# LayerNorm 2 writes its features in an order of five blocks of 2x64, and the gate and up weights are loaded in the same row order

## The chip, the cores and the metric

One core of a Trainium2 chip. The metric is the device time of one execution in microseconds (us), the median of several runs. Engines in the profile: PE is TensorE, PEld its weight loads, DVE is VectorE, ACT is ScalarE, POOL is GpSimd, and SP is the engine that issues nearly all DMA transfers, SPq its queue. In the names, `ps` is a bank in which PE leaves its results, `pa` and `pd` hold the softmax exponents made by ACT and by DVE (with GpSimd's adds), and a product `ps<-qT,kT` makes scores.

## The reference

A transformer block with one key and value head, and a gated feed-forward part, in bf16:

```python
x  : [1, 2048, 640]          # 32 query heads of 20, one K and one V head
h  = x + attention(layernorm(x)) @ wo          # softmax(q k^T / sqrt(20)) v
h2 = h + (gelu(LN(h) @ w_gate) * (LN(h) @ w_up)) @ w_down      # 640 -> 1536 -> 640
# all weights ~ N(0,1) * 0.05; w_gate, w_up, w_down also * (rows ** -0.5)
```

Both LayerNorms are without scale and shift. The product `LN(h) @ w_gate` sums over the 640 features, so the features may stand in any order as long as the rows of the weights stand in the same one.

## The kernel before

The kernel is built by a greedy planner. It keeps a modelled clock for each engine, takes the next task that its model says can start, and so fixes the order of every engine's instructions when the program is built. On the chip each engine works through its own list and waits on semaphores (DVE's stop of 6.53 us below shows what that can cost). A modelled duration that is wrong makes no wrong result. It only makes an order that doesn't suit the chip, and any changed figure can change the order of everything after it.

The normalise step of both LayerNorms (`ln` is 0 or 1, `t` the tile of 128 rows; 16 tiles each):

```python
tk = _Task(("dve",), None, 420, L_DVE, keys + [("lr", kk)], [], prio, then, gate)   # 420 ns in the plan
def bind():
    s = start()
    tk.fn = lambda e: e.tensor_scalar(xn_tmp[:, s, :].rearrange("p (a b) -> p a b", a=5),
                xh[:, t, :], mv[:, ln, t, 0:1], ln_r[:, ln, t:t + 1], ALU.subtract, ALU.mult)
    tk.writes = [("xt", s)]
...
# then a DMA transposition [128 rows, 640] -> [128, 5, 128 rows], issued by SP
sp_tasks.append(_Task(("sp",), lambda e: e.dma_start_transpose(o, xn_tmp[:, s, :]), ...))
```

A task with `lock` set is planned as one that needs GpSimd idle: it starts after the GpSimd instruction in flight, and GpSimd's next starts after it. No wait is emitted for it.

```python
def commit(self, eng, fn, cost, lat, reads=(), writes=(), at=0.0, dma=False, lock=False):
    ...
    t0 = max([self.free[eng], at] + [o.vis for o in deps])
    if lock:
        for o in self.ops["pool"][-2:]:
            if o.t0 <= t0 < o.end:
                t0 = o.end
        self.port = t0 + cost
    elif eng == "pool":
        t0 = max(t0, self.port)
    ...
```

The weights of the output and feed-forward products come in pieces, one after the other: each piece is planned, and waits on the chip, until the piece before it has landed. All are issued by SP:

```python
w_pieces = []
for nm, o, v, n in (("wo", wo_sb, A_wo, 2), ("wg", wg_sb, B_w_gate, 4), ("wu", wu_sb, B_w_up, 4), ("wd", wd_sb, B_w_down, 4)):
    rows = o.shape[1]                       # wg_sb, wu_sb: [128 partitions, 5, 1536]
    cut = [rows * i // n for i in range(n + 1)]
    w_pieces += [(nm, i, o[:, x:y, :], cview(v)[:, x:y, :]) for i, (x, y) in enumerate(zip(cut, cut[1:]))]
for k, (nm, i, o, v) in enumerate(w_pieces):
    sp_tasks.append(_Task(("sp",), (lambda o, v: lambda e: e.dma_start(o, v))(o, v), 560, W_LAT,   # W_LAT = 3000 ns
        [w_pieces[k - 1][:2]] if k else [], [(nm, i)], ...))     # reads the key of the piece before
```

The softmax here doesn't subtract the row's maximum and nothing guards it: scores larger than these inputs give would overflow.

## Time and profile before

| | before |
|---|---|
| median, six runs | 775.96 us (774.23 to 776.50) |
| profiled run | 775.0 us |
| first exponent on ACT starts, last one ends | 13.86 us, 745.78 us |
| ACT busy between these, idle between these | 711.28 us, 20.65 us |
| after ACT's last exponent | 29.25 us |

ACT computes most of the softmax exponents, DVE with GpSimd the others. The four parts (until the first exponent, busy, idle, after the last exponent) add up to the span. They are summed over all records of ACT in the trace. The busy shares, the time lines of one LayerNorm pair and the durations of the line that changes are shown in the prediction.

### The profile page before, as it was taken

To read this page: it belongs to the slowest core of one execution; us is meant where nothing else is said; L and a number is where in the kernel's file an instruction comes from. 1 tells how busy PE (TensorE), PEld (TensorE's weight loads), DVE (VectorE), ACT (ScalarE), POOL (GpSimd) and SP (SyncE) were. 2 spreads that over 40 slices of the span, in tenths; PEclk is the share of its full clock that TensorE was granted. 3 is DMA by queue.
4 is the path that set the end of the run, shared out by engine and by line. 5 is a ranking of instruction groups with operands and counts; after the bars stand their busy time and mean duration, and the time that the engine had idled before them with its cause. 6 is when DMAs were issued, how large, how long until landed. Compare 5 with 4: busy or idle time off the path is not lost.

```text
span 775.0 us, 29498 instructions
## 1 busy us (share of the span) xinstructions
PE 709.2 (92%) x12913; PEld 336.3 (43%) x12913; DVE 614.9 (79%) x1112; ACT 723.7 (93%) x1079; POOL 667.1 (86%) x723
## 2 busy tenths in 40 slices
PE   4788988999999999999989899999998989989998
PEld 3333333343335444455334444454543545434467
DVE  7878888887798888878897777967778787787863
ACT  5799999999999999999999999999998999999961
POOL 4499999989999998888999998878988899999840
PEclk9899999999999999999999999999999999999999
DMA  7544301100101002100100002010031000210000
GB/s 200 92 122 151 110 8 22 23 10 8 25 10 25 9 3 43 26 26 10 26 18 17 3 9 44 17 36 9 4 43 25 9 10 3 44 26 18 11 19 19
DMA packets 56767, 25.87 MB, mean 33 GB/s; under 512 B 47808, under 2 KB 55360, under 8 KB 56640
## 3 DMA queue, kind: packets, MB, share of 16 engines
q1 hardware_dynamic: 55328, 23.55, 13.6%
q8 instruction: 103, 1.69, 0.9%
q10 hardware_dynamic: 1312, 0.44, 0.2%
q14 instruction: 24, 0.20, 0.1%
HBM read 10.21 MB, written 2.62 MB: 17 GB/s over the span
## 4 chain that ended last, share of the span: by engine, by line
PE 56%; ACT 29%; DVE 12%; DMA 2%; issue 1%; DVEq 0%
ACT pa L1625 25%; PE ps L584 21%; PE ps L1345 16%; PE ps L1261 15%; DVE pd L1718 6%; PE ps L580 3%; ACT gbuf L962 2%; DVE xn_tmp L532 2%; DVE osb L1372 1%; DMA xn1T<-xn_tmp 1%; DVE stats L457 1%; DMA xh<-in_A_x_dram 1%; PE ps L1484 1%; ACT L1625 1%; ACT L962 1%
## 5 line engine op out<-in xcount | busy, mean ns | idle before, releaser
L1625 ACT ACTIVATE pa<-ps 128x512 bf16<-128x512 f32 (+1 forms) x1032 | 678.2, 806 | 20.3 <-PE ps L1261 12.9
L1692 POOL TENSOR_TENSOR pd<-pd,shifts 128x512 int32<-128x512 int32 x586 | 595.7, 1040 | 60.9 <-DVE pd L1718 57.2
L1718 DVE TENSOR_SCALAR pd<-ps 128x512 uint16<-128x512 f32 x636 | 422.1, 687 | 121.7 <-PE ps L1261 113.7
L1345 PE MATMUL ps<-pd,v_ext 128*32 128x512 bf16 x1908 | 294.6, 384 | 15.4 <-DVE osb L1372 11.6
L1345 PE MATMUL ps<-pa,v_ext 128*32 128x512 bf16 x1412 | 258.5, 386 | 1.1 <-ACT pa L1625 0.6
L1261 PE MATMUL ps<-qT,kT 32*128 32x512 bf16 x2048 | 221.1, 386 | 32.2 <-DVE pd L1718 15.2
L1261 PEld LDWEIGHTS ps<-qT,kT 32*128 32x128 bf16 x2048 | 61.2, 91 | 203.5 <-DVE pd L1718 108.4
L1345 PEld LDWEIGHTS ps<-pd,v_ext 128*32 128x32 bf16 x1908 | 81.1, 95 | 77.2 <-issue 33.0
L1345 PEld LDWEIGHTS ps<-pa,v_ext 128*32 128x32 bf16 x1412 | 69.7, 95 | 42.3 <-issue 26.2
L584 PE MATMUL ps<-xn2T,wg_sb 128*32 128x256 bf16 x1680 | 65.6, 274 | 0.6 <-DVE gbuf L935 0.5
L584 PE MATMUL ps<-xn2T,wu_sb 128*32 128x256 bf16 x1680 | 64.4, 274 | 1.4 <-DVE qT L654 0.8
L584 PE MATMUL ps<-wd_sb,gbuf 128*32 128x320 bf16 x1252 | 61.8, 301 | 0.1
L584 PE MATMUL ps<-xn1T,wq_pad 128*32 128x256 bf16 (+1 forms) x1440 | 53.2, 265 | 0.1
L584 PEld LDWEIGHTS ps<-xn2T,wg_sb 128*32 128x32 bf16 x1680 | 41.9, 96 | 19.2 <-issue 11.0
L584 PEld LDWEIGHTS ps<-xn2T,wu_sb 128*32 128x32 bf16 x1680 | 41.6, 96 | 17.9 <-issue 9.3
L584 PEld LDWEIGHTS ps<-wd_sb,gbuf 128*32 128x32 bf16 x1252 | 32.6, 96 | 21.8 <-issue 10.7
L584 PEld LDWEIGHTS ps<-xn1T,wq_pad 128*32 128x32 bf16 x1440 | 34.1, 98 | 15.7 <-issue 9.5
L979 DVE TENSOR_TENSOR gbuf<-ps,gbuf 128x512 bf16<-128x512 f32 x48 | 32.8, 684 | 8.5 <-PE ps L580 5.2
L1674 POOL TENSOR_TENSOR pd<-pd,shifts 128x256 int32<-128x256 int32 x48 | 32.3, 689 | 0.0
L457 DVE BATCH_NORM_STATS2 stats<-xh 128x6 f32<-128x320 bf16 x64 | 29.9, 480 | 1.8 <-DMA xh<-in_A_x_dram 1.5
L584 PE MATMUL ps<-wo_sb,onT 128*32 128x320 bf16 x600 | 29.8, 301 | 0.8 <-DVE gbuf L979 0.6
L935 DVE CAST gbuf<-ps 128x512 bf16<-128x512 f32 x42 | 28.8, 687 | 1.3 <-PE ps L584 0.9
(75 smaller groups left out, 347.7 us busy)
## 6 DMA issues: line engine op xcount, KB each, us to landing
out_dram<-xh SPq DMA_DIRECT2D x16, 160.0 KB, 1.8
xh<-in_A_x_dram SPq DMA_DIRECT2D x3, 640.0 KB, 6.7
wd_sb<-in_B_w_down_dram SPq DMA_DIRECT2D x4, 480.0 KB, 3.7
wg_sb<-in_B_w_gate_dram SPq DMA_DIRECT2D x3, 384.0 KB, 3.1
wu_sb<-in_B_w_up_dram SPq DMA_DIRECT2D x3, 384.0 KB, 3.1
wg_sb<-in_B_w_gate_dram SPq DMA_DIRECT2D x1, 768.0 KB, 4.2
wu_sb<-in_B_w_up_dram SPq DMA_DIRECT2D x1, 768.0 KB, 4.4
wo_sb<-in_A_wo_dram SPq DMA_DIRECT2D x1, 480.0 KB, 3.9
```

Of the source, the lines that this page charges most:

```text
L457: dve(lambda e: e.bn_stats(stats[:, ln, t, 6 * h:6 * h + 6], xh[:, t, h * HALF:(h + 1) * HALF]), 395, [key], [("st", ln, t, h)], prio, c)
L580: return e.matmul(o(b), l, r, start=st, stop=sp)
L584: ins = e.matmul(o(b)[a, :], l[:, a], r, start=st, stop=sp, tile_position=(0, 32 * j))
L935: dve(lambda e: e.tensor_copy(o, i), c_dve(n * k), [("b", bk)], ks, 1.0, fin)
L962: task(("act",), (lambda v: lambda e: e.activation(v, v, ACT.Gelu_apprx_tanh))(v), ("gelu", c_act(n * (f1 - f0))), L_ACT, ks, ks, 1.0, (la ...
L979: dve(lambda e: e.tensor_tensor(o, i, o, ALU.mult), c_dve(n * k), [("b", bk)] + ks, ks, 1.0, fin)
L1261: ins = e.matmul(bank(b), kT4[32 * r:32 * r + 32, kt * P:(kt + 1) * P], qT[32 * r:32 * r + 32, s, :], start=True, stop=True, tile_position ...
L1345: ins = e.matmul(ps[32 * r:32 * r + 32, ab * 512:(ab + 1) * 512], v_ext[:, it["kt"], it["w"], :], it["ap"], start=st, stop=(j in ends), ti ...
L1625: op = plan.commit("act", lambda e: e.activation(dst, src, ACT.Exp, scale=SM_SCALE), cost, L_ACT, [("b", b0 + i) for i in range(n)], [("pa ...
L1674: return e.tensor_tensor(pd32[:, w, h], pd32[:, 0, h], shifts[:, w - 1:w].to_broadcast([P, 256 * k]), ALU.add)
L1692: return e.tensor_tensor(pd32[:, 1:3, h], pd32[:, 0, h].unsqueeze(1).to_broadcast([P, 2, 256 * k]), shifts[:].unsqueeze(2).to_broadcast([P ...
L1718: op = plan.commit("dve", lambda e: e.tensor_scalar(pd[:, 0, s * 512:(s + 1) * 512], bank(b), CH_A, CH_B, ALU.mult, ALU.add), c_dve(512), ...
```

## The change

The intent: the normalise of LayerNorm 2 and GpSimd hold each other up. In the trace of the kernel before it takes 814 ns in the mean, against a median of 440 in the head, and six of the GpSimd adds that are in flight when it starts take 1115 to 1171 ns, where an add otherwise takes 1040. This is called the lock below. Its output is now written in an order of blocks, so that neither waits for the other, at the price of a longer instruction where GpSimd is idle (429 to 448 ns now). That a write in blocks does both was the expectation. Since the transposition behind it moves what is written, the 640 features then stand in another order, and the rows of `w_gate` and `w_up` must be loaded in that order. LayerNorm 1's normalise stays as it is, but is now planned as locked, and the planner's figure for a change of ACT's table goes from 1283 to 1520 ns.

```diff
-            tk = _Task(("dve",), None, 420, L_DVE, keys + [("lr", kk)], [], prio, then, gate)
+            tk = _Task(("dve",), None, 420 if ln else 320, L_DVE, keys + [("lr", kk)], [], prio, then, gate)
...
-                tk.fn = lambda e: e.tensor_scalar(xn_tmp[:, s, :].rearrange("p (a b) -> p a b", a=5), xh[:, t, :], ...
+                o = xn_tmp[:, s, :]
+                if ln:
+                    o = o.rearrange("p (h r i) -> p r h i", h=2, r=NC_D)        # 5 x 2 x 64
+                tk.fn = lambda e: e.tensor_scalar(o, xh[:, t, :], ...
...
+            tk.lock = ln == 0
...
-    for nm, o, v, n in (("wo", wo_sb, A_wo, 2), ("wg", wg_sb, B_w_gate, 4), ("wu", wu_sb, B_w_up, 4), ...
+    HP = P // 2
+    half_rows = (lambda a: a.rearrange("(k p) n -> p k n", p=HP))
+    for nm, o, v, n in (("wo", wo_sb, A_wo, 2), ("wg", wg_sb, B_w_gate, 0), ("wu", wu_sb, B_w_up, 0), ...
+        if n: ...                                                            # as before
+        else:                                                                # pieces of 64 partitions
+            w_pieces += [(nm, i, o[p0:p0 + HP, x:y, :], half_rows(v)[:, k0:k0 + 4 * (y - x) - 3:4, :])
+                         for i, (p0, x, y, k0) in enumerate(((0, 0, 3, 0), (HP, 0, 2, 2), (HP, 2, 5, 1), (0, 3, 5, 3)))]
...
-                cost += 1283.0          # a change of ACT's table, in the plan, two places; in a look-ahead 1300 -> 1540
+                cost += 1520.0
```

The rest of the diff adds switches to the planner (triples of exponents, tweaks by position) that are off in this version.

More of the change, by code (lines that the diff above doesn't have):

```diff
@@ L333, in bass_sequential_preLN__grouped_kv_mqa__glu_gated_geglu__prompt_kernel @@
     allocs.append(ps_cm)
+    ps3 = ps[:].rearrange("p (b n) -> p b n", n=512)
+    pa3 = pa[:].rearrange("p (b n) -> p b n", n=512)
     def bank(b, n=512):
@@ L374, in bass_sequential_preLN__grouped_kv_mqa__glu_gated_geglu__prompt_kernel @@
     PRD = 3
+    TRIPLE = 0
     TH0 = 1500.0
@@ L385, in bass_sequential_preLN__grouped_kv_mqa__glu_gated_geglu__prompt_kernel @@
     WQA = 1
+    TWEAK = {}
     W_LAT = 3000.0
@@ L526, in norm @@
             keys = [("x", t)] if ln == 0 else [("h", t, 0), ("h", t, 1)]
-            tk = _Task(("dve",), None, 420, L_DVE, keys + [("lr", kk)], [], prio, then, gate)
+            tk = _Task(("dve",), None, 420 if ln else 320, L_DVE, keys + [("lr", kk)], [], prio, then, gate)
             def bind():
                 s = start()
-                tk.fn = lambda e: e.tensor_scalar(xn_tmp[:, s, :].rearrange("p (a b) -> p a b", a=5), xh[:, t, :], mv[:, ln, t, 0:1],
+                o = xn_tmp[:, s, :]
+                if ln:
+                    o = o.rearrange("p (h r i) -> p r h i", h=2, r=NC_D)
+                tk.fn = lambda e: e.tensor_scalar(o, xh[:, t, :], mv[:, ln, t, 0:1],
                                                   ln_r[:, ln, t:t + 1], ALU.subtract, ALU.mult)
                 tk.writes = [("xt", s)]
+            tk.lock = ln == 0
             tk.born = bind
@@ L1055, in bass_sequential_preLN__grouped_kv_mqa__glu_gated_geglu__prompt_kernel @@
               [("sh", w)], 1.5)
+    HP = P // 2
     w_pieces = []
-    for nm, o, v, n in (("wo", wo_sb, A_wo, 2), ("wg", wg_sb, B_w_gate, 4), ("wu", wu_sb, B_w_up, 4),
+    half_rows = (lambda a: a.rearrange("(k p) n -> p k n", p=HP))
+    for nm, o, v, n in (("wo", wo_sb, A_wo, 2), ("wg", wg_sb, B_w_gate, 0), ("wu", wu_sb, B_w_up, 0),
                         ("wd", wd_sb, B_w_down, 4)):
-        rows = o.shape[1]
-        cut = [rows * i // n for i in range(n + 1)]
-        w_pieces += [(nm, i, o[:, x:y, :], cview(v)[:, x:y, :]) for i, (x, y) in enumerate(zip(cut, cut[1:]))]
+        if n:
+            cut = [o.shape[1] * i // n for i in range(n + 1)]
+            w_pieces += [(nm, i, o[:, x:y, :], cview(v)[:, x:y, :]) for i, (x, y) in enumerate(zip(cut, cut[1:]))]
+        else:
+            w_pieces += [(nm, i, o[p0:p0 + HP, x:y, :], half_rows(v)[:, k0:k0 + 4 * (y - x) - 3:4, :])
+                         for i, (p0, x, y, k0) in enumerate(((0, 0, 3, 0), (HP, 0, 2, 2), (HP, 2, 5, 1), (0, 3, 5, 3)))]
     W_KEYS = {nm: [(nm, i) for n2, i, _, _ in w_pieces if n2 == nm] for nm in ("wo", "wg", "wu", "wd")}
@@ L1134, in pairs_of, with triples_of @@
         return al + un
+    def triples_of(fb):
+        return [[a, a + d, a + 2 * d] for d in (1, 2, 3) for a in fb if a + d in fb and a + 2 * d in fb]
     def act_end():
@@ L1147, in dve_load, with tw @@
         return v + min(m, MISCMAX)
+    def tw(kind, d):
+        return TWEAK.get((kind, state["npack"]), d)
     def stall(t, n, fb):
@@ L1180, in issue_qk @@
         if state["tab"] == "gelu" or any(tk.engs[0] == "act" for tk in tasks):
-            A += sum(tk.cost[1] for tk in tasks if tk.engs[0] == "act" and isinstance(tk.cost, tuple)) + 1300.0
+            A += sum(tk.cost[1] for tk in tasks if tk.engs[0] == "act" and isinstance(tk.cost, tuple)) + 1540.0
         nf = pd_free.count(True) - len(dve_q)
@@ L1195, in issue_qk @@
             n = 1
-        n = max(0, min(n, nf))
+        n = max(0, min(tw("n", n), nf))
         k = state["npack"]
@@ L1213, in issue_half @@
             n = 0
-        n = max(0, min(n, nf))
+        n = max(0, min(tw("a" if more else "b", n), nf))
         return issue_rows(t, u, kt, rows, n, fb, more)
@@ L1231, in issue_rows @@
         units_a = []
+        if tw("t", TRIPLE) and nr == 4 and n == 1:
+            tr = triples_of(fb)
+            if tr:
+                units_a.append(tr[0])
+                fb = [b for b in fb if b not in tr[0]]
+                want = 0
         for _ in range(want):
@@ L1240, in issue_rows @@
         fb.sort(key=lambda b: ((b ^ 1) in fb, b))
-        ns = nr - n - 2 * len(units_a)
+        ns = nr - n - sum(len(x) for x in units_a)
         dbanks = [fb.pop(0) for _ in range(n)]
@@ L1390, in pe_decide @@
         cand = half or next_pack(t)
-        piece = next_piece(t)
+        piece = None if tw("m", 0) else next_piece(t)
         state["misc_ready"] = piece is not None
@@ L1416, in pe_decide @@
                 tq = est[1] if len(est) > 1 else 1e12
-            elif HALF_ON and len(ok) >= 2 and light(t) and tq + 445.0 - act_end() > HGAIN and state["npack"] > HBEG and state[
-                    "tab"] == "exp":
+            elif len(ok) >= 2 and state["npack"] > HBEG and state["tab"] == "exp" and tw(
+                    "h", HALF_ON and light(t) and tq + 445.0 - act_end() > HGAIN):
                 k = state["npack"]
@@ L1422, in pe_decide @@
                 return True
-        lim = max(tq, act_end() - 570.0)
+        lim = max(tq, act_end() - 570.0) + tw("l", 0.0)
         qs = pv_rounds(t)
@@ L1603, in act_decide @@
             s = None
-            if n == 2:
+            ds = 1
+            if n == 3:
+                fr = [i for i in range(NA) if pa_free[i] and plan.ready("act", (), [("pa", i)]) <= t + 20]
+                best = None
+                for d in (1, 2, 3, 4, 5):
+                    for i in fr:
+                        if i + d in fr and i + 2 * d in fr:
+                            q = sum(pa_free[(i + d * j) ^ 1] and ((i + d * j) ^ 1) not in (i, i + d, i + 2 * d)
+                                    for j in range(3))
+                            if best is None or q < best[0]:
+                                best = (q, i, d)
+                if best is not None:
+                    s, ds = best[1:]
+            elif n == 2:
                 for i in range(0, NA, 2):
@@ L1618, in act_decide @@
             b0 = tl[0]["b"]
-            src = ps[:, b0 * 512:(b0 + n) * 512]
-            dst = pa[:, s * 512:(s + n) * 512]
+            db = tl[1]["b"] - b0 if n > 1 else 1
+            if n == 3:
+                src = ps3[:, b0:b0 + 2 * db + 1:db, :]
+                dst = pa3[:, s:s + 2 * ds + 1:ds, :]
+            else:
+                src = ps[:, b0 * 512:(b0 + n) * 512]
+                dst = pa[:, s * 512:(s + n) * 512]
             cost = c_act(512 * n)
@@ L1623, in act_decide @@
                 state["tab"] = "exp"
-                cost += 1283.0
+                cost += 1520.0
             op = plan.commit("act", lambda e: e.activation(dst, src, ACT.Exp, scale=SM_SCALE), cost, L_ACT,
-                             [("b", b0 + i) for i in range(n)], [("pa", s + i) for i in range(n)], at=t)
+                             [("b", b0 + db * i) for i in range(n)], [("pa", s + ds * i) for i in range(n)], at=t)
             for i, x in enumerate(tl):
+                i *= ds
                 pa_free[s + i] = False
```

## The prediction

> **What bounds the kernel now.** I read the page's busy shares first, then the slices, the busy times by stretch, and the groups of the line that changes.
>
> ```profile
> PE 709.2 (92%) x12913; PEld 336.3 (43%) x12913; DVE 614.9 (79%) x1112; ACT 723.7 (93%) x1079; POOL 667.1 (86%) x723
> ACT  5799999999999999999999999999998999999961
> ...
> sum 775.00, PE 709.24 PEld 336.34 DVE 614.90 ACT 723.70 POOL 667.14; mean PE 59.10 PEld 28.03 DVE 51.24 ACT 60.31 POOL 55.60
> ```
>
> ACT is the bound, but only between head and tail. From the stretches between 60 and 740 us, ACT's busy times (79.32, 99.07, 98.00, 98.27, 96.98, 96.81, 58.66, 19.95, 19.36) add up to 666.4 of 680 us: 13.6 us of idle ACT are all that anything can win there without taking work from ACT. The head (0 to 60 us) has 15.2 us of idle ACT, the last 35 us have 22.5. PE, at 92%, is close behind, so ACT's queue of scores is never long.
>
> The line that changes is the normalise instruction of both LayerNorms (L532), 16 times each. Cut at 140 us the two answers are
>
> ```profile
> L532 DVE TENSOR_SCALAR xn_tmp<-xh,mv,ln_r x16: 395/440/942, 6.1 to 37.5; 128x640 bf16<-128x640 bf16 x16
> ...
> L532 DVE TENSOR_SCALAR xn_tmp<-xh,mv,ln_r 128x640 bf16<-128x640 bf16 x16 | 12.7, 814 | 0.1
> ```
>
> The same instruction on the same shape takes 440 ns (median) in the head and 814 ns (mean) as LayerNorm 2. The time lines of one pair show what the extra time is, and what it costs:
>
> ```profile
> 591.48 2.11 DVE L532 TENSOR_SCALAR xn_tmp<-xh,mv,ln_r 128x640 bf16<-128x640 bf16 x2
> ...
> 590.29 3.11 POOL L1692 TENSOR_TENSOR pd<-pd,shifts 128x512 int32<-128x512 int32 x3
> ...
> 594.35 0.39 PE L1261 MATMUL ps<-qT,kT 32*128 32x512 bf16 x4 [1.27 <-DVE pd L1718]
> ...
> 594.80 2.49 ACT L1625 ACTIVATE pa<-ps 128x512 bf16<-128x512 f32 x4 [0.81 <-PE ps L1261]
> 598.15 2.25 ACT L1625 ACTIVATE pa<-ps 128x512 bf16<-128x512 f32 x3 [0.86 <-PE ps L1261]
> ```
>
> Two normalisations occupy DVE for 2.11 us, and GpSimd runs its adds back to back beneath them. DVE's next exponent (L1718) is late, so its score bank is late, PE waits 1.27 us for it, and ACT runs dry for 0.81 and 0.86 us. Set against each other one by one, 12 of the 16 start while a GpSimd instruction has 0.4 to 1.1 us left and end 0.16 to 0.2 us after it; the four that meet none take 429 to 448 ns.
>
> [...] Before, the result is one run of 640[...]. In the changed program it is 5x2x64 against 640[...]. [...] In this trace the exponent, which reads PSUM, keeps to 687 ns beside a GpSimd that is 86% busy[...].
>
> **The change, part by part.** (a) LayerNorm 2's normalise: [...] DVE is 79% busy[...]; the path through the late bank counts. A pair, followed by the next exponent, holds DVE for 1.5 to 2.1 us now[...].
>
> What that is worth on ACT: I listed ACT's gaps over 0.1 us in the 7 us after the start of each LayerNorm 2 pair. After 145 us 0.17 + 0.21; 230: 0.13 + 0.23; 320: 0.26 + 0.39; 403: 0.43; 501: 1.48; 591: 0.81 + 0.86; 687: none; after 725: 0.39. Sum 5.4 us of the 13.6. Not all of it is the lock[...]. [...]I give back about two thirds: **-3.5 us**.
>
> (b) [...]LayerNorm 1's normalise is marked as one that needs GpSimd idle, and an ACT table load costs 1520 in place of 1283 ns in the plan. That moves nothing by itself, but the whole static order is built anew (5753 lines of difference on PE). Comparing the two built streams: ACT loses one exponent of 1024 and one of 512 (380 to 379 and 652 to 651), DVE gains the three tiles (636 to 639), PE does six more value products net (1412 + 1908 = 3320 to 3326). ACT's starts lie 904 and 478 ns apart in a busy row, so 1.38 us less; one osb copy less (0.5), one qT copy more (0.5), small kT and v_ext copies about even: **-1.4 us**. The table loads stay twelve, LayerNorm instructions and fillers (288) stay as many.
>
> (c) Tail: four `wd_sb` products more run in the full-width form after the last exponent (71 to 75). At 320 columns they come about 0.13 us apart there: **+0.5 us**. The last normalise (756.4 us) has an idle GpSimd today and takes 448 ns[...].
>
> (d) Weights: gate and up come in pieces of 64 partitions. [...] 6 x 3.1 + 4.2 + 4.4 = 27 us measured now. [...]gate weights are first used at 154, up weights at 254.7, down weights at 277.9. Hidden: **0**.
>
> (e) Head: LayerNorm 1's normalise is one of the head's inputs to the keys, and its delay until GpSimd is free in the plan can move ACT's first exponents by up to about a microsecond; only 850 ns of lock wait are in the 16 of the head today. I put **0, plus or minus 2**.
>
> Sum: -3.5 - 1.4 + 0.65 + 0 = **-4.3 us**, to 771.7. The rebuilt order should also hold a little better, since the waits that upset it are now foreseen; I take 0.7 us more: **771 us**.
>
> **Rivals.** First, replanning luck: each kernel is one outcome of a greedy scheduler, and 13.6 us of idle in the middle can grow as well as shrink. For it: nearly every row moves, and the settings tuned to the old order are kept. Against it: the middle is already 98% full, so there is more to spoil than to win, and the engines' work is as good as equal. It would give anything from 766 to 779. [...] Third, the lock may be cheap because ACT's gaps come from PE's own blocks (at 506 us, ACT's longest gap, 1.48 us, stands behind a block of 32 down products): then (a) is worth 1 us and the time is about 774. Fourth, more drops than I count: GpSimd also lost about 0.1 us at each collision (1.11 to 1.17 us where an add otherwise takes 1.04) and PE's clock fell to 0.50 in 596 to 598 us after its idle; if all 5.4 us return and the order settles, 767.
>
> **Range and chances.** The mechanism can give at most 5.4 + 1.4 us, so over 2% (15.5 us) needs luck larger than the middle's whole idle time; slower by over 2% needs a stall that the streams don't show. Eight in ten: 765 to 777. Chances: faster 0.04, same 0.94, slower 0.02.
>
> **What would show it.** Right: LayerNorm 2's normalise[...] with little spread[...], none ending on a GpSimd add; [...]adds beside them at 1.04 us; ACT's gaps after the pairs under about 2 us in sum; ACT's exponents about 1.4 us less busy; gate and up landings longer but all landed before 110 us. Wrong: [...]still a spread of 430 to 1250; ACT's idle between 60 and 740 us at or above 13.6 us although the collisions are gone, which would mean that the new order gave them back; a longer head, first seen in ACT's first two slices; or a tail over 36 us.

The parts of the forecast came to -3.5 - 1.4 + 0.65 + 0 = -4.3 us, and with 0.7 us for a steadier order to 771 us. Passages that rested on figures which no run of this case had shown are cut: what the new form and the narrow pieces were to take, with them the second rival, and in (c) a term of 0.15 us, so that the +0.65 is the +0.5 that still stands and that term.

## More of the kernel before

After a unit of attention is done, its output `osb` is transposed into `onr`, VectorE takes the reciprocal of the softmax sums that lie in it, and the rest is normalised:

```python
tk.fn = lambda e: e.dma_start_transpose(onr[:, s, :].rearrange("p (j i) -> p j i", j=4), osb[:, so, :])   # SP
tk.fn = lambda e: e.reciprocal(rcp[:, sr, :].rearrange("p (j r) -> p j r", j=4), v4[:, :, :, Dh])          # DVE, waits for it
```

## The result, and the profile after

| | before | after |
|---|---|---|
| median, six runs each | 775.96 us (774.23 to 776.50) | 782.41 us (780.39 to 783.26) |
| ratio | | 1.0082, 95% interval 1.0064 to 1.0099 |

A ratio is the mean time of one kernel's runs over the mean time of the other's of the same rounds, so it is not quite the ratio of the medians. The change costs 0.8%, some 6.4 us. That is "same" by the 2% rule, as was called most likely, but it lies outside my range of 765 to 777, and the sign is wrong.

**What was aimed at happened.** The groups of instructions, LayerNorm 2's normalise in the changed kernel (minimum, median and maximum in ns, first and last start):

```profile
L540 DVE TENSOR_SCALAR xn_tmp<-xh,mv,ln_r x16: 574/598/607, 147.1 to 760.9; 128x640 bf16<-128x640 bf16 x16
```

598 ns at the median and little spread (574 to 607), where the mean was 814 before. The time line of the pair at 598 us (start, duration, engine, instruction; no bracket means that the engine was not idle before it):

```profile
598.10 0.57 DVE L540 TENSOR_SCALAR xn_tmp<-xh,mv,ln_r 128x640 bf16<-128x640 bf16 x1
...
599.29 0.60 DVE L540 TENSOR_SCALAR xn_tmp<-xh,mv,ln_r 128x640 bf16<-128x640 bf16 x1
...
596.99 2.09 POOL L1740 TENSOR_TENSOR pd<-pd,shifts 128x512 int32<-128x512 int32 x2
...
597.39 6.11 ACT L1672 ACTIVATE pa<-ps 128x512 bf16<-128x512 f32 x9
```

GpSimd's adds run on over the first of the two at 1.04 us each, and ACT goes through nine exponents without a gap. Over all eight pairs ACT's gaps over 0.1 us in the 7 us after a pair's start sum to 1.07 us, 5.35 before.

**Where the time came from.** The slices of ACT in the page of the changed kernel show one new dent, in the fifth of the 40 slices (78 to 97 us):

```profile
ACT  5799699999999999999999999999999999999951
```

The chain that ended last, by engine, first before and then after:

```profile
PE 56%; ACT 29%; DVE 12%; DMA 2%; issue 1%; DVEq 0%
```

```profile
PE 63%; ACT 15%; DVE 15%; DMA 6%; issue 1%; POOL 0%; SPq 0%
```

DMA has gone from 2 to 6% of the path that sets the end. The same chain in the stretch from 60 to 90 us, piece by piece (start, duration, what):

```profile
58.28 5.59 DMA wg_sb<-in_B_w_gate_dram
...
63.88 4.14 DMA wg_sb<-in_B_w_gate_dram
...
68.04 5.49 DMA wu_sb<-in_B_w_up_dram
...
73.55 4.29 DMA wu_sb<-in_B_w_up_dram
...
77.85 0.60 SPq L1081
...
78.49 5.51 DMA onr<-osb
...
84.02 0.25 DVE rcp L762
84.28 0.56 DVE pd L1766
...
84.97 0.61 PE ps L1290 x4
```

This is how the stop comes about. Weight pieces follow each other, each issued when the one before has landed (0.01 to 0.02 us later in this chain). In SP's list the transposition `onr<-osb` stands behind the issue of the next piece, the third of `wu_sb`, so it goes out at 78.49. It then takes 5.51 us and lands 0.46 us behind that piece (issued at 77.85, landed at 83.54; the transposition at 84.00). DVE, which runs in order, stands before the reciprocal of what it brings, and an exponent (`pd`) behind the reciprocal can't start. PE waits for the bank of that exponent, and ACT for PE. What each engine says of it (the bracket is its idle time before the instruction, and what ended it):

```profile
84.02 0.25 DVE L762 RECIPROCAL rcp<-onr 128x16 f32<-128x16 bf16 x1 [6.53 <-DMA onr<-osb]
...
84.97 0.61 PE L1290 MATMUL ps<-qT,kT 32*128 32x512 bf16 x4 [6.71 <-DVE pd L1766]
...
85.63 2.12 ACT L1672 ACTIVATE pa<-ps 128x512 bf16<-128x512 f32 x3 [6.28 <-PE ps L1290]
```

In the kernel before, SP's and DVE's time lines at the same place read:

```profile
61.73 6.23 SPq L1066 DMA_DIRECT2D wu_sb<-in_B_w_up_dram  x3
72.11 1.20 SPq L799 DMA_TRANSPOSE onr<-osb  x1
73.35 0.58 SPq L1066 DMA_DIRECT2D wu_sb<-in_B_w_up_dram  x1
...
77.34 0.24 DVE L753 RECIPROCAL rcp<-onr 128x16 f32<-128x16 bf16 x1
```

There the transposition went out 6.4 us earlier, when the third piece of `wu_sb` had already landed (at 70.76). It took 2.45 us, and DVE did not wait at all (no bracket). The DMA issues of the two kernels give the reason (how many, KB each, median us from issue to landing), before and after:

```profile
wg_sb<-in_B_w_gate_dram SPq DMA_DIRECT2D x3, 384.0 KB, 3.1
...
wg_sb<-in_B_w_gate_dram SPq DMA_DIRECT2D x1, 768.0 KB, 4.2
```

```profile
wg_sb<-in_B_w_gate_dram SPq DMA_DIRECT2D x2, 576.0 KB, 5.5
...
wg_sb<-in_B_w_gate_dram SPq DMA_DIRECT2D x2, 384.0 KB, 4.3
```

384 KB took 3.1 us over 128 partitions and take 4.3 over 64. The stretch of the stop (busy us and instructions of PE, PEld, DVE, ACT and POOL, then PE's granted clock, DMA share, GB/s):

```profile
78.00:84.00 6.00, 0.26 (x4) 0.00 (x0) 0.00 (x0) 1.35 (x3) 0.00 (x0) 0.79 0.68 120
84.00:86.00 2.00, 1.03 (x10) 0.27 (x10) 1.76 (x4) 0.37 (x1) 1.64 (x2) 0.50 0.37 78
```

But for the last 1.35 us of ACT's work and 0.26 us of PE's everything stands, and PE comes back at half its clock (0.50).

SP's list has the transposition in the same place in both kernels, between the third and the fourth piece of `wu_sb`. The built programs, before on the left and after on the right:

```
DMACopy wu_sb <- w_up  128x1536   x3      DMACopy wu_sb <- w_up  64x3x1536
                                          DMACopy wu_sb <- w_up  64x2x1536
                                          DMACopy wu_sb <- w_up  64x3x1536
DmaTranspose onr <- osb 128x4x128         DmaTranspose onr <- osb 128x4x128
DMACopy wu_sb <- w_up  128x2x1536         DMACopy wu_sb <- w_up  64x2x1536
```

So the stop can be worked out from the landings. Before, the seven pieces from the first of `wg_sb` to the third of `wu_sb` took from 48.06 to 70.76 us, 22.7 us; after, from 48.40 to 83.54 us, 35.1 us. Behind the piece in flight the transposition landed 0.46 us later. Before, DVE came to the reciprocal at 77.34 us, so the series of pieces had 77.34 - 70.76 - 0.46 = 6.1 us to spare. It became 12.8 us later: 6.7 us too late. DVE's wait is 6.53 us.

The balance of ACT, for these two kernels and for two of the experiments that follow (us, profiled runs; the span is the sum of the time to the first exponent, busy, idle and after the last exponent; the columns between split the idle time by where it lies):

| | span | to first exponent | busy | idle | of it before 60 | 60 to 140 | 140 to 240 | after 240 | after last exponent |
|---|---|---|---|---|---|---|---|---|---|
| before | 775.0 | 13.86 | 711.28 | 20.65 | 6.87 | 0.68 | 0.93 | 12.17 | 29.25 |
| before_form_only | 770.7 | 14.21 | 710.69 | 16.58 | 6.19 | 0.68 | 0.59 | 9.12 | 29.24 |
| after_old_pieces | 774.2 | 12.77 | 711.56 | 19.76 | 5.99 | 1.04 | 4.14 | 8.59 | 30.11 |
| after | 779.5 | 13.88 | 711.14 | 24.36 | 6.51 | 7.50 | 2.17 | 8.18 | 30.12 |

### The profile page after: what moved, and what is told of

Read it like the earlier page. It is cut to its first block, busy times and chain, and to the rows that moved or that the text cites. A ratio compares the mean times of both kernels' runs of the same rounds, so it can differ in the third digit from the quotient of the medians.

```text
span 779.5 us, 29487 instructions
## 1 busy us (share of the span) xinstructions
PE 712.7 (91%) x12907; PEld 335.9 (43%) x12907; DVE 619.9 (80%) x1120; ACT 723.3 (93%) x1078; POOL 663.1 (85%) x726
## 4 chain that ended last, share of the span: by engine, by line
PE 63%; ACT 15%; DVE 15%; DMA 6%; issue 1%; POOL 0%; SPq 0%
PE ps L593 23%; PE ps L1374 19%; PE ps L1290 17%; ACT pa L1672 12%; DVE pd L1766 8%; PE ps L589 3%; DMA wg_sb<-in_B_w_gate_dram 3%; DVE osb L1401 2%; ACT gbuf L971 1%; DMA wu_sb<-in_B_w_up_dram 1%; DVE xn_tmp L540 1%; DVE stats L461 1%; DMA wo_sb<-in_A_wo_dram 1%; DVE qT L663 1%; DMA onr<-osb 1%
## 5 line engine op out<-in xcount | busy, mean ns | idle before, releaser
L1672 ACT ACTIVATE pa<-ps 128x1024 bf16<-128x1024 f32 (+1 forms) x1030 | 677.6, 807 | 24.1 <-PE ps L1290 18.2
L1740 POOL TENSOR_TENSOR pd<-pd,shifts 128x512 int32<-128x512 int32 x572 | 580.8, 1038 | 58.3 <-DVE pd L1766 54.8
L1290 PE MATMUL ps<-qT,kT 32*128 32x512 bf16 x2048 | 220.4, 386 | 35.1 <-DVE pd L1766 19.4
L593 PE MATMUL ps<-xn2T,wg_sb 128*32 128x256 bf16 x1680 | 63.8, 274 | 0.6 <-DVE gbuf L944 0.5
L593 PE MATMUL ps<-wd_sb,gbuf 128*32 128x320 bf16 x1236 | 60.2, 301 | 0.2 <-DVE gbuf L988 0.2
L593 PEld LDWEIGHTS ps<-xn2T,wg_sb 128*32 128x32 bf16 x1680 | 41.1, 96 | 17.7 <-issue 10.4
L1722 POOL TENSOR_TENSOR pd<-pd,shifts 128x256 int32<-128x256 int32 x65 | 44.0, 696 | 0.0
L593 PE MATMUL ps<-wo_sb,onT 128*32 128x320 bf16 x600 | 31.7, 301 | 0.2
L486 POOL TENSOR_TENSOR ln_den<-ln_ve,halfc 128x2 bf16<-128x2 bf16 (+1 forms) x18 | 11.9, 662 | 21.0 <-DVE ln_ve L479 21.0
```

The costliest lines, as they stand in the source:

```text
L486: task(("pool",), lambda e: e.tensor_tensor(ln_den[:, ln, sl], ln_ve[:, ln, sl], halfc[:, 0:n], ALU.pow), 690, L_POOL, [("ve", kk), "halfc ...
L593: ins = e.matmul(o(b)[a, :], l[:, a], r, start=st, stop=sp, tile_position=(0, 32 * j))
L1290: ins = e.matmul(bank(b), kT4[32 * r:32 * r + 32, kt * P:(kt + 1) * P], qT[32 * r:32 * r + 32, s, :], start=True, stop=True, tile_position ...
L1672: op = plan.commit("act", lambda e: e.activation(dst, src, ACT.Exp, scale=SM_SCALE), cost, L_ACT, [("b", b0 + db * i) for i in range(n)], ...
L1722: return e.tensor_tensor(pd32[:, w, h], pd32[:, 0, h], shifts[:, w - 1:w].to_broadcast([P, 256 * k]), ALU.add)
L1740: return e.tensor_tensor(pd32[:, 1:3, h], pd32[:, 0, h].unsqueeze(1).to_broadcast([P, 2, 256 * k]), shifts[:].unsqueeze(2).to_broadcast([P ...
```

## The experiments

The theory after the first look: the stop at 78 to 84 us, made by the weight pieces of 64 partitions, is the loss. The rivals: the rebuilt order costs time by itself, or the new form of the write costs somewhere what it gains at the pairs. Every kernel ran five rounds beside the kernel before, in three batches, in which the kernel before had medians of 776.64, 776.33 and 776.57 us (11 runs each). I compared the built programs row by row: after_wide_loads, after_two_port and after_old_pieces have the order of the changed kernel, and before_narrow_loads, before_one_port, before_form_only and before_blocks_backwards that of the kernel before. In each, the lists of PE, ACT and GpSimd have the same work in the same order; only the form of the normalise, or the loads in SP's list, differ, and in before_blocks_backwards 2880 products of PE read another chunk of the transposed tile. The other four have orders of their own. "One port" and "two port" in the labels are names for the write in blocks and the contiguous write; no trace here shows ports.

### after_wide_loads: the changed kernel, the reordered rows loaded over 128 partitions

```diff
-            w_pieces += [(nm, i, o[p0:p0 + HP, x:y, :], half_rows(v)[:, k0:k0 + 4 * (y - x) - 3:4, :]) ...]
+    # block c of 128 rows = rows 64*LO[c].. and 64*HI[c]..; one load with DRAM dims [2 halves, 64 rows, 1536]
+    return [(o[:, c, :], bass.AP(v.tensor, at(LO[c]), [[(HI[c] - LO[c]) * 64 * n, 2], [n, 64], [1, n]]))]
```

> The changed kernel with its order of instructions untouched on PE, ACT, DVE and GpSimd; only the gate and up pieces are fetched 128 partitions at a time (the same permuted rows, correct result). Theory (slow pieces): the changed kernel lost 6.3 us at 79 us, where VectorE stood in front of a reciprocal until an attention transpose landed that sat in SP's queue behind 64-partition weight pieces of 4.1 to 5.7 us each. With pieces of about 3 us that gap goes to under 0.5 us, and the time falls from 782.4 by 5 to 7 us, to 775 to 777. Rival (replanning): the new static order is the worse one all along its length; then the gap at 79 us moves elsewhere or is made up later, and the time stays at 780 or above.

Measured: 829.61 us (827.52 to 832.47), ratio 1.0681 [1.0656, 1.0706]. The expectation failed, through my own experiment. The pieces took about 10.4 us for 384 KB (from one issue to the next), and one stretch of it reads:

```profile
92.00:102.00 10.00, 0.00 (x0) 0.00 (x0) 0.00 (x0) 0.00 (x0) 0.00 (x0) 0.63 0.11 39
```

A DMA share of 0.11 of 16 engines is the time of 1.8 engines, at 39 GB/s. No run varies the loads' pattern of two halves alone, so why they are slow was not shown. The run says nothing about loads without a cost. It does show the same cause in an overdose: DVE stood 11.5, 27.2 and 13.6 us before three reciprocals, each waiting for an attention transposition that stood in SP's list behind slow or delayed pieces.

### before_narrow_loads: the kernel before, its rows in the old order, in pieces of 64 partitions

```diff
+            hr = v.rearrange("(k p) n -> p k n", p=P // 2)
+            w_pieces += [(nm, i, o[p0:p0 + P // 2, x:y, :], hr[:, k0 + 2 * x:k0 + 2 * y - 1:2, :])
+                         for i, (p0, x, y, k0) in enumerate(((0, 0, 3, 0), (64, 0, 2, 1), (64, 2, 5, 1), (0, 3, 5, 0)))]
```

> The kernel before, its order untouched; only the gate and up pieces are fetched as 64 partitions by 3 or 2 chunks, rows in their old order (correct). Theory (slow pieces): its second attention transpose also stands behind three up pieces, and its reciprocal came at 77.3 us with the transpose landed at 74.6, so 2.8 us of slack against about 9 us by which the pieces run late: a stop of about 5 to 7 us near 77 us and 781 to 783 in place of 776. Rival (replanning): the loads are hidden in either kernel, 776 within 1.

Measured: 785.94 us (784.73 to 786.62), ratio 1.0115 [1.0096, 1.0133], 9.3 us more than before. The stop is there, with nothing else of the change:

```profile
86.14 0.25 DVE L753 RECIPROCAL rcp<-onr 128x16 f32<-128x16 bf16 x1 [6.68 <-DMA onr<-osb]
```

The transposition was issued at 80.59 and landed at 86.11, again just behind the piece ahead of it (85.67). So the loads alone make the stop. They cost more here than I expected: ACT's idle time from 60 to 140 us is 8.05 us (0.68 before), of which a second wait of DVE, 1.07 us at 106 us, again before a reciprocal, is a part, and the first exponent starts 1.96 us later (15.82 against 13.86 us) in this profiled run.

### before_one_port: the kernel before, with the new form, and the wide loads of the first experiment

```diff
-   xn_tmp[:, s, :].rearrange("p (a b) -> p a b", a=5)
+   xn_tmp[:, s, :].rearrange("p (h r i) -> p r h i", h=2, r=NC_D) if ln else xn_tmp[:, s, :]
    # and the loads of after_wide_loads
```

> The kernel before, its order untouched; the second LayerNorm writes 5x2x64 as in the changed kernel and the permuted rows are fetched 128 partitions at a time[...] (correct). This is the intent of the change alone. Theory: the normalise takes 598 ns as in the changed kernel, ACT's gaps after the pairs shrink from 5.4 to 1 to 2 us, and the time falls by 3 to 5 us to 771 to 773. Rival (the lock costs nothing, gaps are PE's own): 775 to 777.

Measured: 828.61 us (827.80 to 829.73), ratio 1.0667 [1.0647, 1.0686]. The bad loads (those of after_wide_loads, about 10.4 us for 384 KB there) cover everything, so it is inconclusive on the worth of the form. It is asked again below.

### after_two_port: the changed kernel's order and narrow loads, with the old contiguous write

```diff
-                if ln:
-                    o = o.rearrange("p (h r i) -> p r h i", h=2, r=NC_D)
     # rows in their natural order, still in pieces of 64 partitions
```

> The changed kernel, its order and its 64-partition pieces untouched; only the second LayerNorm writes 640 in a row again, and the rows come in their old order (correct). Theory: the normalise is back at 700 to 850 ns with a spread up to 1.25 us, ACT's gaps after the pairs are back at 4 to 6 us, and the stop at 79 us stays: 785 to 788 in place of 782.4. Rival (the lock costs nothing): 782 within 1.

Measured: 787.90 us (784.30 to 790.47), ratio 1.0136 [1.0111, 1.0161]: 0.54 points, about 4.2 us, above the changed kernel. The collisions are back:

```profile
L536 DVE TENSOR_SCALAR xn_tmp<-xh,mv,ln_r x16: 431/604/1270, 148.3 to 767.7; 128x640 bf16<-128x640 bf16 x16
```

ACT's gaps after the pairs sum to 3.29 us, less than the 4 to 6 expected. The form is worth about as much in the new order as in the old one (next but one). The rival that it costs elsewhere what it gains falls.

### after_old_pieces: the changed kernel with the loads of the kernel before (rows wrong)

```diff
-            w_pieces += [(nm, i, o[p0:p0 + HP, x:y, :], half_rows(v)[:, k0:k0 + 4 * (y - x) - 3:4, :]) ...]
+            w_pieces += [(nm, i, o[:, x:y, :], cview(v)[:, x:y, :]) for i, (x, y) in enumerate(((0, 1), (1, 2), (2, 3), (3, 5)))]
```

The features are then multiplied with the wrong rows; every instruction stays in its place.

> The changed kernel, order untouched on every engine; the gate and up weights are fetched exactly as in the kernel before (128 partitions, pieces of 1, 1, 1 and 2 chunks, rows in the old order), so the result is WRONG on purpose: features and rows no longer match. This replaces after_wide_loads, whose loads came out slower than those it was to speed up (10 us a piece). Theory (slow pieces): pieces land in 2.8 to 4.4 us again, VectorE's 6.5 us stop before the reciprocal goes to under 0.5 us, and 782.4 falls to 774 to 777. Rival (the new order is the worse one): 780 or more.

Measured: 775.95 us (774.88 to 778.48), ratio 0.9998 [0.9981, 1.0015]. SP's and DVE's lines:

```profile
70.27 1.21 SPq L808 DMA_TRANSPOSE onr<-osb  x1
...
75.82 0.24 DVE L762 RECIPROCAL rcp<-onr 128x16 f32<-128x16 bf16 x1
```

The transposition goes out 8.2 us earlier than in the changed kernel, and the reciprocal has no wait. The loads cost the changed kernel 1.0082 - 0.9998 = 0.0084 of 776 us, 6.5 us.

### before_form_only: the kernel before, with nothing but the new form (rows wrong)

```diff
-   xn_tmp[:, s, :].rearrange("p (a b) -> p a b", a=5)
+   xn_tmp[:, s, :].rearrange("p (h r i) -> p r h i", h=2, r=NC_D) if ln else xn_tmp[:, s, :]
```

> The kernel before, order and loads untouched; only the second LayerNorm writes 5x2x64, so the result is WRONG on purpose (rows not permuted). Theory: normalise at 598 ns, ACT's gaps after the pairs from 5.4 to 1 to 2 us, 776.6 falls to 771 to 774. Rival (the collisions cost no time): 776 to 777.

Measured: 772.52 us (772.11 to 773.58), ratio 0.9952 [0.9938, 0.9965]: 3.7 us less.

```profile
L532 DVE TENSOR_SCALAR xn_tmp<-xh,mv,ln_r x16: 524/597/606, 144.7 to 752.1; 128x640 bf16<-128x640 bf16 x16
```

This is step (a) of the prediction, alone: predicted -3.5 us, measured -3.7. The balance puts most of it in ACT's idle time after 240 us (12.17 to 9.12), and ACT's gaps after the eight pairs fall from 5.35 to 2.28 us, a little above the 1 to 2 expected. 1.27 us of what is left is the gap near 505 us, 1.48 before: that one was not the lock's.

The difference from after_old_pieces is the rebuilt order alone (form and loads are alike): 0.9998 - 0.9952 = 0.0046, 3.6 us **more**. In the balance of the two profiled runs it is 3.55 us of idle ACT from 140 to 240 us, 0.87 us of busy ACT and 0.87 us after the last exponent; against them the first exponent came 1.44 us earlier, and the rest is small. PE and DVE in after_old_pieces, at its longest wait in that stretch:

```profile
176.80 0.79 DVE L1715 TENSOR_SCALAR pd<-pd 128x1024 uint16<-128x1024 uint16 x1
177.51 0.68 DVE L1400 CAST osb<-ps 128x512 bf16<-128x512 f32 x1
...
178.24 0.61 PE L1373 MATMUL ps<-pa,v_ext 128*32 128x512 bf16 x2 [1.27 <-DVE osb L1400]
```

DVE copies a unit's output out of a bank behind an add, PE stands 1.27 us for that bank, and then its clock is half for ten microseconds, though PE is busy (columns as above):

```profile
178.00:180.00 2.00, 1.76 (x14) 0.38 (x18) 1.33 (x3) 1.12 (x3) 1.05 (x2) 0.51 0.34 66
...
186.00:188.00 2.00, 2.00 (x23) 0.36 (x16) 0.96 (x2) 1.56 (x3) 1.85 (x3) 0.50 0.00 0
188.00:190.00 2.00, 1.95 (x27) 0.45 (x23) 1.32 (x3) 1.62 (x4) 2.00 (x3) 0.93 0.00 0
```

In before_form_only the same stretch reads:

```profile
178.00:180.00 2.00, 1.92 (x26) 0.57 (x26) 1.55 (x3) 2.00 (x5) 1.92 (x3) 1.00 0.36 74
...
186.00:188.00 2.00, 2.00 (x31) 0.71 (x31) 1.46 (x3) 2.00 (x4) 2.00 (x4) 1.00 0.00 0
```

PE gets through 23 matmuls where the other order has 31, and ACT starves six times, for 0.88, 0.32, 0.49, 0.49, 0.43 and 0.38 us, 2.99 us together: most of the 3.55.

The wait belongs to the order, but the ten microseconds at half clock do not belong to every run of it. In the changed kernel, whose order on PE and DVE is the same, the wait (1.27 us before 187.16 us) was followed by 3.41 us at half clock, and ACT lost 1.13 us there; in backwards_ln1_lock, below, a like wait was followed by none. Four of the six runs of after_old_pieces have a mean clock of 0.991 and two of 0.996. Those two took 775.0 us on average, the two runs of before_form_only with 0.996 took 773.2. So at equal clock about 1.8 of the 3.6 us remain (an estimate from two runs each); the rest came with more time at half clock.

### before_blocks_backwards: a write in blocks without reordered rows

The five blocks of 128 features are written from the last to the first, and the products read them in that order. The rows of the weights and their loads stay as they were.

```diff
+    def backwards(v):
+        return bass.AP(v.tensor, v.offset + (NC_D - 1) * P, [v.ap[0], [-P, NC_D], [1, P]])
-   xn_tmp[:, s, :].rearrange("p (a b) -> p a b", a=5)
+   backwards(xn_tmp[:, s, :]) if ln else xn_tmp[:, s, :]
-   xn2T[:, c, x0:x0 + n]
+   xn2T[:, NC_D - 1 - c, x0:x0 + n]
```

> The kernel before, order and loads untouched; the second LayerNorm writes its five blocks of 128 features from the last to the first[...], and the gate and up products read the transposed chunks in the opposite order, so no weight row moves. Correct. Theory: [...]the normalise takes about 600 ns as with 5x2x64, and the time is that of before_form_only, 771 to 774: the change's gain without its cost. [...]

Measured: 773.73 us (771.36 to 775.68), ratio 0.9965 [0.9947, 0.9983]: 2.7 us less than before.

```profile
L532 DVE TENSOR_SCALAR xn_tmp<-xh,mv,ln_r x16: 524/597/607, 143.8 to 751.0; 128x640 bf16<-128x640 bf16 x16
```

The same duration as the 5x2x64 form, and no change to the loads at all. The gain is 2.7 us against 3.7 for that form, and the intervals overlap: within the noise, the gain of the idea can be had this way. By the reference's scales the feed-forward branch is some 6e-5 beside a residual of 0.05 (an estimate), so the comparison can't see the order of the rows. That this kernel is right rests on its reasoning: chunk 4 - c of the transposed tile holds the features of block c, and is multiplied with block c of the weights.

### after_true_latency: the changed kernel, and the planner told what the narrow pieces take

```diff
+    def w_lat(o):
+        return W_LAT if o.shape[0] == P else (5000.0 if o.shape[1] == 3 else 3900.0)
-   ..., 560, W_LAT, ...
+   ..., 560, w_lat(o), ...
```

> The changed kernel with one thing more: the planner is told that a weight piece of 64 partitions lands 5.0 us (3 chunks) or 3.9 us (2 chunks) after issue and not 3.0, so it makes a new order (correct). Theory: the reciprocal and the transposes are placed where the transposes really land, VectorE's stop goes to under 1 us, and the time is 773 to 778. Rival (a planner that knows only delays the same work): 780 to 784.

Measured: 782.49 us (780.40 to 784.53), ratio 1.0074 [1.0054, 1.0094]. The stop is gone. The transposition now stands behind the first piece of `wu_sb` in place of the third, and landed at 75.55 us (that piece at 74.89). The reciprocal starts at 77.6 us without a wait, and ACT idles 0.60 us from 60 to 140 us, though the pieces are as narrow as in the changed kernel. So in this stretch the narrow pieces did harm only through what stood behind them. But the expectation failed: the order is another one, and gives the time back later. (No run moves the transposition alone and leaves the rest of the order as it was.) ACT in this kernel:

```profile
760.46 0.60 ACT L946 ACTIVATE gbuf<-ps 128x512 bf16<-128x512 f32 x1 [7.78 <-PE ps L589]
```

After the last exponent 32.96 us pass (30.12 in the changed kernel), and ACT's idle time after 240 us is 12.01 us (8.18).

### backwards_table_cost, backwards_ln1_lock, before_lock_planned: what in the planner's new figures costs

The first adds the two table figures to before_blocks_backwards, the second the lock of LayerNorm 1 instead. The third is the kernel before with its contiguous write, but both LayerNorms planned as locked.

```diff
# backwards_table_cost                    # backwards_ln1_lock                    # before_lock_planned
-  cost += 1283.0                         -  ..., 420, L_DVE                      -  ..., 420, L_DVE
+  cost += 1520.0   # and 1300 -> 1540    +  ..., 420 if ln else 320, L_DVE       +  ..., 320, L_DVE
                                          +  tk.lock = ln == 0                    +  tk.lock = True
```

> before_blocks_backwards (fast loads, [...]order of the kernel before, 773.7) with the planner's cost of an ACT table load raised from 1283 to 1520 ns and 1300 to 1540 ns, as in the change; it makes a new order. Correct. Theory A (the new order of the changed kernel costs 3.5 us because a truer plan is systematically worse here): 776 to 778. Theory B (an order is a draw: the same amounts of work end within some us of each other, whatever the constant says): anywhere in 769 to 779, with ACT's busy time within 1 us of 711 and the difference in ACT's idle and in the tail.

Measured: 772.46 us (770.36 to 775.50), ratio 0.9944 [0.9921, 0.9968], the lowest of all kernels here that compute the right thing: 4.3 us below the kernel before by its ratio, and ahead of the changed kernel by some 10 us. Against before_blocks_backwards the intervals overlap, so the two figures cost nothing and may be worth a microsecond.

> backwards_table_cost with the first LayerNorm's normalise marked as one that needs GpSimd idle, at 320 ns, as in the change: this is the changed kernel's planning with fast loads, and its order should be that of the changed kernel but for what the slower pieces' keys move. Correct. Theory A: equal to after_old_pieces, 775 to 777. Theory B: also about 776 if the order comes out the same, else anywhere in 769 to 779.

Measured: 776.17 us (773.97 to 778.86), ratio 0.9990 [0.9967, 1.0012], some 2 us above before_blocks_backwards. The expectation speaks of both changes, but the kernel that ran has the lock alone: its table figures are still 1283 and 1300. So it is not the changed kernel's planning, and its order is another one. Both theories allowed this time, so it doesn't decide between them. PE's wait for the copy of a unit's output is here too, and ACT loses 0.45 us behind it:

```profile
180.08 0.39 PE L1350 MATMUL ps<-pa,v_ext 128*32 128x512 bf16 x2 [1.28 <-DVE osb L1377]
...
180.86 10.14 ACT L1630 ACTIVATE pa<-ps 128x512 bf16<-128x512 f32 x17 [0.45 <-PE ps L1266]
```

But PE's clock stays at 1.00, and what is more here is ACT's busy time (713.0 us against 710.43). The order built with the lock of LayerNorm 1 comes with a loss of some 2 us, part of it in the same place, most of it not.

> The kernel before with both normalises [...]marked as ones that need GpSimd idle, at 320 ns: the other cure for the collisions, with the lock planned and not avoided; loads as before. Correct. Theory: the collisions go (normalises at 430 to 450 ns, or few above), ACT's gaps after the pairs fall to 1 to 3 us; the new order is a draw on top: 768 to 779, centre 774. Rival (GpSimd held idle for the lock costs adds): 778 or more.

Measured: 777.53 us (776.76 to 778.91), ratio 1.0008 [0.9989, 1.0027].

```profile
L532 DVE TENSOR_SCALAR xn_tmp<-xh,mv,ln_r x16: 417/628/1165, 140.4 to 755.6; 128x640 bf16<-128x640 bf16 x16
```

The expectation that the collisions go failed. A plan that keeps the two engines apart doesn't keep them apart on the chip: 417 to 1165 ns, a mean of 701 against 814; no wait is emitted for the lock. ACT's gaps after the pairs did fall, to 2.01 us, and its idle time from 20.65 to 18.78 us, but the time after the last exponent rose from 29.25 to 31.38 us. In these runs the form of the write that needs no lock did better than the plan that knows of it; the orders differ, so the two are not compared alone.

## Why the prediction was wrong

The steps along one line, each from a ratio: form alone 0.9952 (-3.7 us), rebuilt order 0.9998 (+3.6 us), narrow loads 1.0082 (+6.5 us). That they add up to the measured +6.4 us is so by construction, each being the step from the ratio before. In another order they have other sizes: on the kernel before the narrow loads cost 8.9 us (1.0115). Of the signs of being wrong that the prediction named, one came true: ACT's idle time between 60 and 740 us rose from 13.58 to 17.52 us although the collisions were gone, and is 13.60 us in after_old_pieces, so without the slow loads the new order gave back what the form had won.

- **(a) The lock: right.** 598 ns measured, and the same beside a busy GpSimd: in the changed kernel 15 of the 16 start with a GpSimd instruction in flight that has 0.09 to 0.98 us left, and take 574 to 607 ns; the one that meets none takes 606; the adds among them take 1.03 to 1.04 us. -3.5 us predicted, -3.7 measured; that the two thirds came so close is partly luck, since ACT's gaps after the pairs fell by 3.07 us. With a write in blocks (after, before_form_only, before_blocks_backwards) all durations lie within 524 to 607 ns, with a contiguous write (before, after_two_port, before_lock_planned) they spread over 417 to 1270 ns. The rival of a cheap lock falls, but for the one gap near 505 us.
- **(d) The weights, "Hidden: 0": this step failed.** The gate and up pieces all landed by 88 us, as I had asked for, and it was the wrong question. I had asked when the weights are first read, not what else stands in the queue that carries them. The transposition stood there in the kernel before as well, in the built program, with 6.1 us to spare. How little it took is seen from the slack: over the seven pieces ahead it is 0.9 us a piece (an estimate, 6.1 / 7), and 384 KB alone took 1.2 us more over 64 partitions than over 128 (4.3 against 3.1). before_narrow_loads shows the cause alone, after_old_pieces its absence, after_true_latency that the place in the queue is what matters.
- **(b) The rebuilt order, -1.4 us and -0.7 us for settling: the sign was wrong.** ACT's busy time between first and last exponent is 711.28 before and 711.14 after, so the 1.4 us of work that I counted out of the streams didn't come as a shorter path; the exponents themselves are 0.6 us less busy (678.2 to 677.6). In place of the gain, the order cost 3.6 us, about half of it with time at half clock that not every run has (the estimate above). And the planner was not told the truth all round: its new 1520 ns for a table load stand against 1283 in the traces. My first rival, the luck of a greedy planner, had said that there is more to spoil in the middle than to win (I had put this among the reasons against it); I gave it room in the range, and yet put a gain into the sum. In the changed kernel itself the stop at 84 us shifts what follows, and idle time from 140 to 240 us is 2.17 us rather than 4.14.
- **(c) The tail: right in kind.** +0.65 us predicted, +0.87 measured.
- **(e) The head: 0, right.** The first exponent starts at 13.88 us (13.86 before), and ACT idles 6.51 us until 60 us (6.87). That LayerNorm 1's normalise is planned with the lock did not help it: its 16 durations sum to 9.3 us, 7.8 before, with three above 1.1 us. The plan's lock missed here too.

What stays open: whether marking LayerNorm 1 as locked is bad as a rule. The two orders built with that mark, a write in blocks and no slow loads (after_old_pieces and backwards_ln1_lock, 776.0 and 776.2 us) both lost some or all of what the form gained. Both have PE's wait of 1.27 or 1.28 us for the copy of a unit's output, but the time lies for the most part elsewhere, and two are few. Open too is why the same wait is followed by half clock in one run and not in another.

## What to carry to other kernels

Before a transfer is called hidden, ask not only when its data is first used but also what is issued behind it on the same queue, and who waits for that. When a layout change forces a new access pattern on loads, look for a layout that has the wanted property and leaves the loads alone: five blocks written backwards gave the same 597 ns, and the gain within the noise. And in a program with a planned order, time the idea on the old order first, and count any replanning as a draw, not as a gain.

## What these runs show of the hardware

- Pieces of 64 partitions in the changed kernel took 5.4 to 5.7 us (576 KB) and 4.1 to 4.4 us (384 KB) from issue to landing; the 192 KB between the two sizes took 1.2 us, about 164 GB/s beside other traffic (an estimate from these medians). Over 128 partitions, in the kernel before, 384 KB took 3.1 us at the median.
- A transposition issued behind a piece of 64 partitions landed 0.44 to 0.66 us after that piece in each of eight cases (four kernels), so 2.45 us became 3.49 to 5.52. The width is not needed for it: behind a 480 KB piece of 128 partitions, issued 0.4 to 1.2 us before it, it landed 0.46 to 0.65 us after that piece in four cases (the same kernels), 3.35 to 4.16 us after its own issue.
- The normalise that writes 5x2x64 took 598 ns at the median (after) and 597 (before_form_only); written as 5x128 with a block step of -128 and a unit step inside (before_blocks_backwards) it took the same 597 ns.
- In after_old_pieces half clock followed a wait of PE of 1.27 us and lasted some 10 us (0.50 to 0.51), with PE busy for 1.76 to 2.00 of every 2 us. Such a wait need not do it: between 60 and 740 us the thirteen traces hold 18 waits of PE of 1.26 to 1.46 us, and half clock came within 3.6 us of the end of six of them.
